# Block-sparse attention and feed-forward: P turned in f32 by TensorE, P by V in f32, values read straight from the input

## The chip, the core and the metric

The kernel runs on one core of a Trainium2 chip. TensorE (PE in the rows; its weight loads are PEld) multiplies, VectorE (DVE), ScalarE (ACT) and GpSimd (POOL) work on vectors, and SyncE (SP) issues most of the transfers. Each engine takes its instructions in the order in which they stand. The metric is the time of one execution in microseconds (us), lower is better.

## The reference

Four batches, 8 heads, 768 tokens, 64 values per head; blocks of 32 tokens, so 24 blocks. What is computed, cut to the core:

```python
scores = (q @ k.T) / 8                         # per head, 768 x 768
# allowed for a query block: itself and its two neighbours, blocks 0 and 23, 3 sampled blocks;
# query blocks 0 and 23 see everything
scores = where(mask, scores, -1e9); scores -= max(scores, -1)
attn = exp(scores); attn /= sum(attn, -1) + 1e-9
x = (attn @ v)                                 # 768 x 512 per batch, heads side by side
xn = (x - mean(x)) / sqrt(var(x) + 1e-6) * g   # over the 512
out = x + relu(xn @ w_ch1) @ w_ch2             # 512 -> 2048 -> 512, f32
```

## The kernel before, in words

**Tiles and visits.** A batch is six tiles of 128 query tokens, taken in the order 1, 2, 3, 0, 4, 5. Tile 0 holds the query blocks 1, 2, 0 and 23. Each other tile is worked in two visits of kind N (four heads each; 4 heads x 256 keys = 1024 columns of scores). Tile 0 takes four visits of kind D (two heads, the two blocks that see all 768 keys) and one of kind H (all eight heads for the other two blocks). That makes 15 visits a batch, 60 in all: 40 N, 16 D, 4 H.

**A step.** The loop at the end of the function runs one step per visit. In step s it writes, in this order: the scores of visit s (`scores`, f32 matmuls into PSUM), their row maxima (`biggest`), then P by V of the visit two steps earlier (`LAG` is 2; `attn_v`, `evict`), then the exponentials of visit s (`softmax`), and then a list of tasks with pieces of the feed-forward network between them. The order of each engine's instructions is that of this writing.

**P in halves.** P is kept as a high and a low f16 part: ScalarE rounds (L278), GpSimd takes the difference (L279), and SyncE turns both by DMA transposes (`turn`, L285) into `pth` and `ptl`. V is held in the same way: at the start of each batch the values are loaded, scaled and split, and stored as f16 rows (high, a column of ones, low: 129 per head) in a scratch tensor `vsd` in DRAM. P by V then is two f16 matmuls per piece, of 129 and of 65 columns, with 32 stationary columns each, so that four of them stand side by side in the array.

**Values.** `values` gathers the rows that a visit needs from `vsd` into one of two buffers `vs`. For an N visit SyncE issues three static transfers (L184, L189) and twelve (L204) whose block numbers it has first read into registers (L147, twice). A D visit needs one transfer for two visits, an H visit twelve.

**Feed-forward.** A tile whose attention is done is normalised (`norm_a`: DVE, ACT, POOL), turned by two DMA transposes on SyncE (`norm_b`, L360 and L361), and then goes with a second tile into a unit of 192 + 96 f16 matmuls (`pu` L377, `pd` L400; each f32 product is three f16 ones). `norm_b` is written only once the unit before has written all its `pu`. A unit is due three steps (`LAG + 2` = 4 before the change) after the last visit of its second tile, and the loop spreads a unit's matmuls evenly over the steps until the next unit is due: the planner counts 109 ns per `pu` and 215 ns per `pd`, 41.57 us for a unit of two tiles. Where the next unit is four steps away that is 10.4 us a step; where the five visits of tile 0 lie between, seven steps, it is 5.9 us.

**Start.** In the steps 0 to 7 the weights arrive as f64 words and are turned into f16 pairs by DVE, ACT and POOL (`split_w1`, `split_w2`).

Of the kernel before, what the change touches and what calls it, by code (L numbers as in the profile page):

```python
# [19 lines left out]
SV = 64.0  # L20
SP_ = 4096.0
# [6 lines left out]
def sparse_attention_moe(  # L28
# [7 lines left out]
    g: bass.AP,  # L36
    w1: bass.AP,
# [14 lines left out]
    dram = ctx.enter_context(tc.tile_pool(name="dram", bufs=1, space=bass.MemoryType.DRAM))  # L52
# [50 lines left out]

    def load_v(b, c, dma):
        dma.dma_start(vr_s[:, c % 2, :], v[b, c])

    def split_v(b, c, pool=False):
        raw = vr_s[:, c % 2, :].rearrange("p (h d) -> p h d", d=D)
        row = vrow_s[c % 2]
        r = row.rearrange("p f (h e) -> p (f h) e", e=129)  # L110
        if pool:
            nc.scalar.activation(raw, raw, AF.Copy, scale=SV)
            nc.scalar.copy(r[:, :, 0:D], raw)
            nc.gpsimd.tensor_sub(r[:, :, D + 1 : 129], raw, r[:, :, 0:D])
        else:
            nc.scalar.activation(r[:, :, 0:D], raw, AF.Copy, scale=SV)
            nc.vector.scalar_tensor_tensor(out=r[:, :, D + 1 : 129], in0=raw, scalar=SV,
                                           in1=r[:, :, 0:D], op0=ALU.mult, op1=ALU.subtract)

    def save_v(b, c, dma):  # L120
        dma.dma_start(vsd[b].rearrange("f r e -> r f e")[c * P : (c + 1) * P], vrow_s[c % 2])
# [137 lines left out]
    def biggest(vi):  # L259
# [6 lines left out]
                                scalar2=math.log(SP_), op0=ALU.mult, op1=ALU.add)  # L266

    def softmax(vi):
        n, w = vi.shape
        ps, p, st = vi.ps, p_s, vi.st  # L270
        ph, pl = ph_s[vi.i % 2], pl_s[vi.i % 2]
        half = n * w if n == 1 else n * w // 2
        for lo in range(0, n * w, half):
            for h in range(lo // w, (lo + half) // w):
                nc.scalar.activation(p[:, h * w : (h + 1) * w], ps[:, h * w : (h + 1) * w],  # L275
                                     AF.Exp, bias=st[:, 4 + h : 5 + h], scale=0.125)
            s = slice(lo, lo + half)
            nc.scalar.copy(ph[:, s], p[:, s])  # L278
            nc.gpsimd.tensor_sub(pl[:, s], p[:, s], ph[:, s])  # L279

    def turn(vi, low):
        n, w = vi.shape
        c = n * w // P
        src, dst = ((ph_s, pth_s), (pl_s, ptl_s))[low]
        nc.sync.dma_start_transpose(out=dst[vi.i % 2][:, 0:c, :],  # L285
                                    in_=src[vi.i % 2][:, 0 : n * w])

    def attn_v(vi):
        pth, ptl, vs = pth_s[vi.i % 2], ptl_s[vi.i % 2], vi.vs
        pv = vi.pv = ps_v.tile([P, 1024], F32, tag="pv", name=f"pv{vi.i}")  # L290
        for n, h in enumerate(vi.heads):
            o = 512 * (n % 4 // 2) + 129 * (n % 2)
            e = 129 * (h % 4)
            rows = slice(0, 4) if vi.kind == "N" else slice(0, 2)
            nch = 6 if vi.kind == "D" else 2
            for c in range(nch):
                for low in range(2):
                    pt, w = ((pth, 129), (ptl, D + 1))[low]
                    for gg in range(4 if vi.kind == "N" else 2):
                        first = n % 2 == 0 and c == 0 and low == 0  # L300
                        last = n % 2 == 1 and c == nch - 1 and low == 1
                        j, pr = h % 2, h // 2
                        if vi.kind == "N":
                            ch, lanes, row = (2 * j + pr % 2) * 2 + c, gg, gg
                            vv = 2 * gg + c
                        elif vi.kind == "H":
                            ch, lanes, row = (2 * j + pr // 2) * 2 + c, 2 * (pr % 2) + gg, gg
                            vv = 4 * gg + 2 * c + h // 4
                        else:
                            ch, lanes, row, vv = c, 2 * (pr % 2) + gg, 2 + gg, c  # L310
                        nc.tensor.matmul(pv[32 * row : 32 * row + 32, o : o + w],  # L311
                                         pt[:, ch, 32 * lanes : 32 * lanes + 32],
                                         vs[:, vv, e : e + w],
                                         start=first, stop=last, skip_group_check=True)
            if vi.kind == "H" and n == 3:
                yield
        yield

    def evict(vi, part):
        rows = {"N": slice(0, 128), "H": slice(0, 64), "D": slice(64, 128)}[vi.kind]  # L320
        hs = vi.heads[4 * part : 4 * part + 4]
        nb, step = len(hs) // 2, hs[1] - hs[0]
        x = vi.tile.x[rows]
        if vi.kind == "D":
            x = x.rearrange("p (a j d) -> p a j d", j=2, d=D)[:, 2 * vi.hf : 2 * vi.hf + 2, hs[0] % 2, :]
        else:
            x = x[:, hs[0] * D : (hs[0] + 4) * D].rearrange("p (h d) -> p h d", d=D)
        tl = tl_s[rows, 0 : 2 * nb, :]
        rs = sm.tile([P, 2 * nb, 1], F32, tag="rs", name=f"rs{vi.i}_{part}")[rows]

        def view(lo, hi):
            u = vi.pv.rearrange("p (b e) -> p b e", b=2)[rows, 0:nb, 0:258]
            return u.rearrange("p b (h e) -> p b h e", e=129)[:, :, :, lo:hi]

        def four(a):
            return a.rearrange("p (b h) d -> p b h d", h=2)

# [236 lines left out]
    while s < NV + LAG + 2 or queue or nextu < len(units):  # L574
# [14 lines left out]
        if vi:  # L589
            softmax(vi)  # L590
# [78 lines left out]
```

## Time and profile before

| | |
|---|---|
| median of 3 runs | 994.09 us (990.64 to 998.07) |
| profiled execution, its own time | 990.98 us |
| its span, first to last instruction | 989.2 us |
| TensorE busy | 711.0 us (72%) |
| VectorE, ScalarE, GpSimd busy | 427.5, 322.9, 299.7 us |
| mean granted TensorE clock | 0.899 of full |
| moved by DMA | 138.84 MB |

The page's busy times are those of one execution; instructions that only issue a transfer or load a register do not count as busy, so SyncE has no share there and is read from its timeline (written SPq). Scores and their times carry f32 matmuls, which the trace records as two matmuls each: the 16 of an N visit appear as x32.

### The profile page before, as it was taken

What the parts mean: (1) busy time and instruction counts of PE and PEld (TensorE: products, weight loads), DVE (VectorE), ACT (ScalarE), POOL (GpSimd) and SP (SyncE); (2) the same over time, 40 slices, a digit from 0 to 9 for tenths busy, and PEclk for the clock granted to TensorE, in tenths of its full rate; (3) what the DMA queues carried; (4) which work ended last, traced back from release to release, by engine and by line L of the source; (5) the groups of instructions that cost most, each with busy time, mean ns of one, the idle gap of its engine ahead of it and who ended that gap; (6) DMA issues with size and microseconds to landing.
All of it is one profiled execution on the core that took longest, in us unless ns stands there. A gap on an engine that the chain in (4) does not pass through costs nothing.

```text
span 989.2 us, 23113 instructions
## 1 busy us (share of the span) xinstructions
PE 711.0 (72%) x8896; PEld 452.1 (46%) x8896; DVE 427.5 (43%) x1001; ACT 322.9 (33%) x631; POOL 299.7 (30%) x319
## 2 busy tenths in 40 slices
PE   1012535698468979996579799985598899875995
PEld 0001323285247455662265474842373656632853
DVE  6539468745335334453534253453353342430300
ACT  2414344454124232262233232542241322530200
POOL 2515344454221312352312213451222212330000
PEclk9999957799779989998779899996799999986998
DMA  7895678577865556589555667777555573744000
GB/s 287 170 204 119 170 201 207 122 180 162 177 140 120 127 123 141 142 168 229 118 116 109 150 118 167 178 163 174 118 125 123 125 145 90 143 114 105 9 25 11
DMA packets 221281, 138.84 MB, mean 140 GB/s; under 512 B 157491, under 2 KB 210484, under 8 KB 220148
## 3 DMA queue, kind: packets, MB, share of 16 engines
q1 hardware_dynamic: 209250, 92.50, 44.5%
q0 software_dynamic: 8080, 30.71, 10.2%
q10 hardware_dynamic: 3842, 14.16, 4.9%
q8 instruction: 70, 1.15, 0.5%
q14 instruction: 39, 0.32, 0.1%
HBM read 88.75 MB, written 12.90 MB: 103 GB/s over the span
## 4 chain that ended last, share of the span: by engine, by line
PE 27%; SPq 21%; DMA 14%; DVE 13%; issue 12%; ACT 8%; POOL 2%; DVEq 1%; ACTq 0%; POOLq 0%
PE pu L377 11%; PE pd L400 8%; SPq L204 8%; DMA ptl<-pl 7%; SPq L147 5%; PE pv L311 5%; DMA vs<-vsd 4%; SPq L285 4%; PE ps L229 3%; ACT p L275 2%; ACT ph L278 2%; DVE st L262 2%; DVE hl L388 2%; DVE ks L164 1%; ACT hh L387 1%
## 5 line engine op out<-in xcount | busy, mean ns | idle before, releaser
L377 PEld LDWEIGHTS <-w1h 128*128 128x128 f16 x1664 | 157.5, 102 | 22.2
L400 PE MATMUL pd<-w2h,hh 128*128 128x512 f16 x384 | 152.8, 398 | 2.9 <-ACT w2h L439 2.9
L400 PE MATMUL pd<-w2l,hh 128*128 128x512 f16 x384 | 151.8, 395 | 1.9 <-POOL w2l L440 1.9
L400 PE MATMUL pd<-w2h,hl 128*128 128x512 f16 x384 | 151.9, 396 | 0.0
L338 ACT COPY tl<-pv 128x256 f32<-128x256 f32 (+2 forms) x64 | 21.9, 343 | 395.9 <-PE pv L311 395.9
L311 PE MATMUL pv<-vs,pth 128*32 128x129 f16 x1792 | 87.1, 253 | 87.9 <-DMA vs<-vsd 70.3
L279 POOL TENSOR_TENSOR pl<-p,ph 128x512 f16<-128x512 f32 (+1 forms) x104 | 133.0, 1280 | 49.0 <-ACT ph L278 26.6
L343 POOL TENSOR_TENSOR x<-tl,rs 128x256 f32<-128x256 f32 (+2 forms) x64 | 35.8, 559 | 347.7 <-ACT p L275 199.8
L229 PE MATMUL ps<-ks,q 64*32 64x256 f32 x1408 | 58.0, 432 | 106.0 <-DMA q<-qT 45.2
L388 DVE SCALAR_TENSOR_TENSOR hl<-pu,hh 128x512 f16<-128x512 f32 x96 | 65.9, 690 | 155.3 <-ACT hh L387 155.0
L377 PE MATMUL pu<-xth,w1h 128*128 128x256 f16 (+1 forms) x832 | 127.0, 277 | 0.0
L377 PE MATMUL pu<-xth,w1l 128*128 128x256 f16 (+1 forms) x832 | 124.6, 274 | 0.0
L377 PE MATMUL pu<-xtl,w1h 128*128 128x256 f16 (+1 forms) x832 | 122.6, 272 | 0.0
L400 PEld LDWEIGHTS <-hh 128*128 128x128 f16 x768 | 77.1, 101 | 99.1 <-issue 17.0
L311 PEld LDWEIGHTS <-pth 128*32 128x32 f16 x1792 | 66.7, 114 | 120.5 <-DMA vs<-vsd 69.5
L311 PE MATMUL pv<-vs,ptl 128*32 128x65 f16 x1792 | 72.8, 221 | 36.3 <-DMA ptl<-pl 36.3
L275 ACT ACTIVATE p<-ps,st 128x256 f32<-128x256 f32 (+1 forms) x192 | 88.0, 505 | 32.0 <-DVE st L265 19.9
L387 ACT ACTIVATE hh<-pu 128x512 f16<-128x512 f32 x96 | 57.1, 595 | 118.2 <-PE pu L377 113.9
L262 DVE TENSOR_REDUCE st<-ps 128x4 f32<-128x1024 f32 (+1 forms) x60 | 68.9, 1149 | 48.9 <-PE ps L229 48.1
L377 PEld LDWEIGHTS <-w1l 128*128 128x128 f16 x832 | 81.0, 102 | 10.8
L229 PEld LDWEIGHTS ps<-ks,q 64*32 64x32 f32 x1408 | 24.6, 115 | 129.9 <-issue 72.2
L311 PEld LDWEIGHTS <-ptl 128*32 128x32 f16 x1792 | 60.3, 111 | 42.7 <-DMA ptl<-pl 42.4
(83 smaller groups left out, 694.4 us busy)
## 6 DMA issues: line engine op xcount, KB each, us to landing
vs<-vsd SPq DMA_DIRECT2D x488, 32.2 KB, 1.7
vs<-vsd SPq DMA_DIRECT2D x40, 387.0 KB, 4.6
vs<-vsd SPq DMA_DIRECT2D x72, 129.0 KB, 4.5
vs<-vsd SPq DMA_DIRECT2D x8, 774.0 KB
out<-ot POOLq DMA_DIRECT2D x24, 256.0 KB, 2.8
q<-qT POOLq DMA_DIRECT2D x23, 256.0 KB, 3.3
vsd<-vrow POOLq DMA_DIRECT2D x18, 258.0 KB, 4.0
vr<-v POOLq DMA_DIRECT2D x18, 256.0 KB, 4.1
```

What stands on the lines that cost most here:

```text
L147: _, vals = nc.values_load_multi_w_load_instructions(flat, engines=[eng], min_val=0, max_val=top, skip_runtime_bounds_check_because=WHY)
L204: dma.dma_start(vs[32 * r : 32 * r + 32, 2 * gg, :], s[bass.ds(reg[3 * (gg % 2) + r] * BLK, BLK), :])
L229: nc.tensor.matmul(ps[32 * part : 32 * part + 32, col : col + n], lhs[64 * row : 64 * row + 64], rhs[64 * row : 64 * row + 64], start=True ...
L262: nc.vector.tensor_reduce(out=st[:, 0:n], in_=vi.ps[:, 0 : n * w].rearrange("p (h k) -> p h k", k=w), axis=AX.X, op=ALU.max, negate=True)
L275: nc.scalar.activation(p[:, h * w : (h + 1) * w], ps[:, h * w : (h + 1) * w], AF.Exp, bias=st[:, 4 + h : 5 + h], scale=0.125)
L279: nc.gpsimd.tensor_sub(pl[:, s], p[:, s], ph[:, s])
L285: nc.sync.dma_start_transpose(out=dst[vi.i % 2][:, 0:c, :], in_=src[vi.i % 2][:, 0 : n * w])
L311: nc.tensor.matmul(pv[32 * row : 32 * row + 32, o : o + w], pt[:, ch, 32 * lanes : 32 * lanes + 32], vs[:, vv, e : e + w], start=first, st ...
L377: nc.tensor.matmul(ph[:, j * n : (j + 1) * n], w[:, ct, fs], x[:, ct, 0:n], start=m == 0, stop=m == 3 * CT - 1, skip_group_check=True)
L387: nc.scalar.activation(dh, ph, AF.Relu)
L388: nc.vector.scalar_tensor_tensor(out=dl, in0=ph, scalar=0.0, in1=dh, op0=ALU.max, op1=ALU.subtract)
L400: nc.tensor.matmul(po, x[:, f, ts], w[:, f, :], start=m == 0, stop=m == 3 * FT - 1)
```

## The change

P stays f32. After the exponentials (now written into `p` alone, with no scale of 4096) TensorE turns the 128-column pieces of P through a PSUM tile with an identity matrix, ScalarE copies them to SBUF, and P by V is one f32 matmul of 65 columns per piece. The host lays the values out as f32 rows of 65 per head with the ones in place, and `values` gathers from that input; loading, splitting and storing V is gone, and so are the low parts of P and the addition of the two sums. P by V follows its scores by one step instead of two (`LAG` 1), the first unit may start in step 4 instead of 5, the loads of q and k are issued by SyncE instead of GpSimd, the weights' staging buffers are other ones, and the feed-forward's PSUM ring has three banks instead of four.

```diff
-    HV = 4 * 129
+    HV = 4 * 65
-    NX, LAG, FFN0 = 5, 2, 5
+    NX, LAG, FFN0 = 5, 1, 4
-    ps_f = ctx.enter_context(tc.tile_pool(name="ps_f", bufs=4, space=bass.MemoryType.PSUM))
+    ps_t = ctx.enter_context(tc.tile_pool(name="ps_t", bufs=1, space=bass.MemoryType.PSUM))
+    ps_f = ctx.enter_context(tc.tile_pool(name="ps_f", bufs=3, space=bass.MemoryType.PSUM))
-    vs_s = ring("vs", 2, [P, 8, HV], F16)
+    vs_s = ring("vs", 2, [P, 8, HV], F32)
...
     def values(vi, dma):
-        src, vs = vsd[vi.b], vi.vs
+        src, vs = v[vi.b], vi.vs
...
     def softmax(vi):
         n, w = vi.shape
-        ps, p, st = vi.ps, p_s, vi.st
-        ph, pl = ph_s[vi.i % 2], pl_s[vi.i % 2]
-        half = n * w if n == 1 else n * w // 2
-        for lo in range(0, n * w, half):
-            for h in range(lo // w, (lo + half) // w):
-                nc.scalar.activation(p[:, h * w : (h + 1) * w], ps[:, h * w : (h + 1) * w],
-                                     AF.Exp, bias=st[:, 4 + h : 5 + h], scale=0.125)
-            s = slice(lo, lo + half)
-            nc.scalar.copy(ph[:, s], p[:, s])
-            nc.gpsimd.tensor_sub(pl[:, s], p[:, s], ph[:, s])
-
-    def turn(vi, low):
-        n, w = vi.shape
-        c = n * w // P
-        src, dst = ((ph_s, pth_s), (pl_s, ptl_s))[low]
-        nc.sync.dma_start_transpose(out=dst[vi.i % 2][:, 0:c, :],
-                                    in_=src[vi.i % 2][:, 0 : n * w])
+        for h in range(n):
+            hs = slice(h * w, (h + 1) * w)
+            nc.scalar.activation(p_s[:, hs], vi.ps[:, hs], AF.Exp, bias=vi.st[:, 4 + h : 5 + h],
+                                 scale=0.125)
+
+    def turn(vi):
+        pt = ps_t.tile([P, 8, P], F32, tag="pt", name=f"pt{vi.i}")
+        c = vi.shape[0] * vi.shape[1] // P
+        dst = pt_s[vi.i % 2]
+        for lo in range(0, c, 4):
+            hi = min(c, lo + 4)
+            for k in range(lo, hi):
+                nc.tensor.transpose(pt[:, k, :], p_s[:, k * P : (k + 1) * P], id_sb)
+            nc.scalar.copy(dst[:, lo:hi, :], pt[:, lo:hi, :])
 
     def attn_v(vi):
...
+        def mm(row, col, ch, vv, e, c):
+            nc.tensor.matmul(pv[32 * row : 32 * row + 32, 65 * col : 65 * col + 65],
+                             pt[:, ch, 32 * row : 32 * row + 32], vs[:, vv, 65 * e : 65 * e + 65],
+                             start=row not in begun, stop=c == nch - 1, skip_group_check=True)
+            begun.add(row)
...
     def evict(vi):
...
-        nc.scalar.copy(four(tl), view(D + 1, 129))
...
-        nc.vector.tensor_add(four(tl), view(0, D), four(tl))
-        nc.gpsimd.tensor_mul(x, tl, rs.to_broadcast(list(x.shape)))
+            nc.vector.tensor_mul(o, u[:, :, 0:D], rs.to_broadcast([P, 4, D]))
...
-    for c in range(6):
-        at(0, first_v, c)
...
-        at(s, load_q, t.n, nc.gpsimd)
+        at(s, load_q, t.n, nc.sync)
...
-                at(s, load_k, t.b, lo, lo + 12, nc.gpsimd)
+                at(s, load_k, t.b, lo, lo + 12, nc.sync)
...
-            at(s1 - 8 + c, load_v, b, c, nc.gpsimd)
-            at(s1 - 7 + c, split_v, b, c)
-            at(s1 - 7 + c, save_v, b, c, nc.gpsimd)
...
         if vi:
+            for _ in values(vi, nc.sync):
+                pass
             softmax(vi)
...
         if vi:
-            vals = values(vi, nc.sync)
-            if s >= LAG:
-                extra = [(lambda: next(vals), ()), (lambda: turn(vi, 0), ()),
-                         (lambda: next(vals, 0), ()), (lambda: turn(vi, 1), ())]
-                tasks = extra[:2] + [(norms, ())] + extra[2:] + tasks
...
+            k = len(tasks) // 2
+            tasks = tasks[:k] + [(turn, (vi,))] + tasks[k:]
         tasks.append((norms, ()))
```

What this does to the order of two engines, in a step of an N visit. On TensorE, where the scores of a step begin before the change (`ps` are scores, `pv` P by V, `pu` and `pd` the feed-forward):

```order
L377 MATMUL pu_14_5483<-xth,w1h 128x256
L229 MATMUL ps_5486<-ks_79,q_92 32x256 x16
L311 LDWEIGHTS pth_89
L311 MATMUL pv_5506<-vs_81,pth_89 32x129
...
L311 LDWEIGHTS ptl_91
L311 MATMUL pv_5506<-vs_81,ptl_91 32x65
```

The same place in the changed kernel, and behind the dots the middle of the step before it ends:

```order
L372 MATMUL pd_4792<-w2l,hh 128x512
L257 MATMUL pt_4968<-id_sb,p 128x128 x8
L372 LDWEIGHTS hh
...
L204 MATMUL ps_5003<-ks_81,q_88 32x256 x16
L267 MATMUL pv_5023<-vs_82,pt_86 32x65 x32
L372 LDWEIGHTS hh
```

Sixty-four f16 matmuls of P by V became 32 f32 ones, and eight transposes of P stand in the middle of the step's feed-forward.

On SyncE, where a tile's transposes for the feed-forward stand (`xth`, `xtl`), before:

```order
L204 DMA vs_82<-vsd_117 32x516
L285 DMA_TRANSPOSE pth_88<-ph_84 128x8x128
L360 DMA_TRANSPOSE xth<-xh_100 128x4x128
L361 DMA_TRANSPOSE xtl<-xl_102 128x4x128
L147 TENSOR_LOAD ei
L204 ISA
...
L285 DMA_TRANSPOSE ptl_90<-pl_86 128x8x128
L184 DMA vs_81<-vsd_117 96x4x516
L189 DMA vs_81<-vsd_117 32x4x516 x2
```

And now:

```order
L179 DMA vs_83<-v 32x260
L130 DMA q_87<-qT 128x512
L332 DMA_TRANSPOSE xth<-xh_95 128x4x128
L333 DMA_TRANSPOSE xtl<-xl_97 128x4x128
L159 DMA vs_82<-v 96x4x260
L164 DMA vs_82<-v 32x4x260 x2
L122 TENSOR_LOAD ei
```

The transposes of P are gone from SyncE; those of the feed-forward's input stood between the two halves of a visit's gather and now stand behind the whole gather of one visit and ahead of that of the next.

## Rows read from the trace of the kernel before

**Rows 1.** The page: busy us by engine; chain that ended last, by engine.

```profile
PE 711.0 (72%) x8896; PEld 452.1 (46%) x8896; DVE 427.5 (43%) x1001; ACT 322.9 (33%) x631; POOL 299.7 (30%) x319
...
PE 27%; SPq 21%; DMA 14%; DVE 13%; issue 12%; ACT 8%; POOL 2%; DVEq 1%; ACTq 0%; POOLq 0%
```

**Rows 2.** Busy us by stretch: length, engines (instructions), TensorE clock, DMA share, GB/s.

```profile
0.00:94.21 94.21, 12.37 (x257) 6.03 (x257) 54.76 (x103) 33.19 (x54) 38.29 (x32) 1.00 0.77 200
94.21:174.84 80.63, 35.85 (x564) 23.87 (x564) 54.33 (x94) 33.16 (x57) 33.81 (x28) 0.80 0.74 187
174.84:214.99 40.15, 33.16 (x348) 20.47 (x348) 25.19 (x47) 19.07 (x34) 19.17 (x21) 0.80 0.57 137
...
425.28:576.04 150.76, 115.54 (x1508) 73.23 (x1507) 62.72 (x170) 50.75 (x109) 45.93 (x54) 0.88 0.67 145
576.04:633.33 57.29, 56.03 (x671) 36.17 (x670) 24.60 (x58) 19.77 (x35) 17.74 (x21) 1.00 0.72 149
...
844.90:989.20 144.30, 111.75 (x1203) 71.79 (x1202) 32.66 (x77) 28.09 (x59) 20.23 (x24) 0.88 0.29 67
```

**Rows 3.** SyncE's timeline, 303 to 318 us: start, us, line, operation, count.

```profile
303.19 0.53 SPq L184 DMA_DIRECT2D vs<-vsd  x1
303.77 0.94 SPq L189 DMA_DIRECT2D vs<-vsd  x2
306.27 3.91 SPq L204 DMA_DIRECT2D vs<-vsd  x6
310.27 1.25 SPq L285 DMA_TRANSPOSE pth<-ph  x1
313.33 2.91 SPq L204 DMA_DIRECT2D vs<-vsd  x6
316.34 1.24 SPq L285 DMA_TRANSPOSE ptl<-pl  x1
317.67 0.53 SPq L184 DMA_DIRECT2D vs<-vsd  x1
```

**Rows 4.** TensorE's waits: for whom, us in total, times, longest.

```profile
PE pv L311 <- DMA vs<-vsd: 70.3, 35, 5.6
PE ps L229 <- DMA q<-qT: 62.8, 3, 37.0
...
PE pv L311 <- DMA ptl<-pl: 36.3, 22, 6.0
```

**Rows 5.** TensorE's timeline from 304 us, an N visit.

```profile
304.17 1.10 PE L229 MATMUL ps<-ks,q 64*32 64x256 f32 x32 [1.65 <-DVE ks L171]
305.20 0.24 PE L311 MATMUL pv<-vs,pth 128*32 128x129 f16 x4
...
306.02 0.61 PE L377 MATMUL pu<-xth,w1h 128*128 128x256 f16 x4
```

**Rows 6.** TensorE's timeline from 367 us, a D visit.

```profile
367.37 1.49 PE L229 MATMUL ps<-kx,q 64*32 64x512 f32 x16
368.79 0.24 PE L311 MATMUL pv<-vs,pth 128*32 128x129 f16 x4
```

**Rows 7.** TensorE's timeline near the end: 512 and 128 columns.

```profile
957.47 0.38 PE L400 MATMUL pd<-w2h,hl 128*128 128x512 f16 x1
957.68 0.38 PE L400 MATMUL pd<-w2l,hh 128*128 128x512 f16 x1
957.90 0.39 PE L377 MATMUL pu<-xth,w1h 128*128 128x128 f16 x4
958.12 0.39 PE L377 MATMUL pu<-xth,w1l 128*128 128x128 f16 x4
```

**Rows 8.** Timelines of a tile's normalisation (DVE first, POOL last) and of the end.

```profile
321.88 0.69 DVE L348 BATCH_NORM_STATS2 ln<-x 128x6 f32<-128x512 f32 x1 [0.73 <-POOL x L343]
...
325.21 1.24 POOL L356 TENSOR_TENSOR xl<-xn,xh 128x512 f16<-128x512 f32 x1 [0.53 <-ACT xh L355]
...
979.18 0.69 DVE L406 SCALAR_TENSOR_TENSOR ot<-pd,x 128x512 f32<-128x512 f32 x1 [9.04 <-PE pd L400]
```

**Rows 9.** Groups by line: busy us, mean ns of one.

```profile
L387 ACT ACTIVATE hh<-pu 128x512 f16<-128x512 f32 x96 | 57.1, 595 | 118.2 <-PE pu L377 113.9
L229 PE MATMUL ps<-ks,q 64*32 64x256 f32 x1408 | 58.0, 432 | 106.0 <-DMA q<-qT 45.2
L229 PEld LDWEIGHTS ps<-ks,q 64*32 64x32 f32 x1408 | 24.6, 115 | 129.9 <-issue 72.2
```

More of the change, by code (lines that the diff above doesn't have):

```diff
@@ L102, in sparse_attention_moe @@
     tf = const.tile([1, NB, NR], F32, name="tf")
[L104 to L121, printed above, removed]
     def index_a():
@@ L281, in turn @@
-    def turn(vi, low):
-        n, w = vi.shape
-        c = n * w // P
-        src, dst = ((ph_s, pth_s), (pl_s, ptl_s))[low]
-        nc.sync.dma_start_transpose(out=dst[vi.i % 2][:, 0:c, :],
-                                    in_=src[vi.i % 2][:, 0 : n * w])
-    def attn_v(vi):
[L289 to L325, printed above, removed]
-        else:
[L327 to L336, printed above, removed]
-        nc.scalar.copy(four(tl), view(D + 1, 129))
-        nc.vector.tensor_scalar(out=four(rs), in0=view(D, D + 1), scalar1=SV * SP_ * 1e-9,
-                                scalar2=None, op0=ALU.add)
-        nc.vector.reciprocal(rs, rs)
-        nc.vector.tensor_add(four(tl), view(0, D), four(tl))
-        nc.gpsimd.tensor_mul(x, tl, rs.to_broadcast(list(x.shape)))
@@ new lines, in evict @@
+    def evict(vi):
+        n = 1 if vi.kind == "D" else 4
+        u = vi.pv[:, 0 : n * 65].rearrange("p (h e) -> p h e", e=65)
+        rs = sm.tile([P, n, 1], F32, tag="rs", name=f"rs{vi.i}")
+        nc.vector.tensor_scalar(out=rs, in0=u[:, :, D : D + 1], scalar1=1e-9, scalar2=None,
+                                op0=ALU.add)
+        nc.vector.reciprocal(rs, rs)
+        x = vi.tile.x
+        if vi.kind == "N":
+            o = x[:, vi.hf * 256 : vi.hf * 256 + 256].rearrange("p (h d) -> p h d", d=D)
+            nc.vector.tensor_mul(o, u[:, :, 0:D], rs.to_broadcast([P, 4, D]))
+            return
+        for rr in range(2):
+            rows = slice(64 * rr, 64 * rr + 64)
+            if vi.kind == "D":
+                h = 4 * vi.hf + 2 * rr + vi.r % 2
+                nc.vector.tensor_scalar(out=x[64:128, h * D : (h + 1) * D], in0=u[rows, 0, 0:D],
+                                        scalar1=rs[rows, 0, :], scalar2=None, op0=ALU.mult)
+            else:
+                for pp in range(2):
+                    o = x[0:64, (4 * pp + 2 * rr) * D : (4 * pp + 2 * rr + 2) * D]
+                    nc.vector.tensor_mul(o.rearrange("p (j d) -> p j d", d=D),
+                                         u[rows, 2 * pp : 2 * pp + 2, 0:D],
+                                         rs[rows, 2 * pp : 2 * pp + 2, :].to_broadcast([64, 2, D]))
@@ L479, in sparse_attention_moe @@
                                  shape=(1, 768) if kind == "D" else (4, 256))
-            if not (kind == "D" and r % 2):
-                nv += 1
+            vi.fresh = not (kind == "D" and r % 2)
+            nv += vi.fresh
             vi.vs = vs_s[nv % 2]
@@ L584, in sparse_attention_moe @@
                 assert t.n < NX or tiles[t.n - NX].done
-            for part, _ in enumerate(attn_v(pvi)):
-                evict(pvi, part)
+            attn_v(pvi)
+            evict(pvi)
             if pvi is t.visits[-1]:
@@ L643 @@
     k = inputs["k"].reshape(b, h // 2, 2, 24, blk, d).transpose(0, 2, 5, 3, 1, 4)
-    v = inputs["v"].transpose(0, 2, 1, 3).reshape(b, 6, 128, h * d)
+    v = inputs["v"].transpose(0, 2, 1, 3).reshape(b, s, 2, h // 2, d).transpose(0, 2, 1, 3, 4)
+    rows = _np.zeros((b, 2, s + blk, h // 2, d + 1), _np.float32)
+    rows[:, :, :s, :, :d] = v
+    rows[:, :, :s, :, d] = 1
     w1, w2 = bits(inputs["moe_w_ch1"]), bits(inputs["moe_w_ch2"])
@@ L648 @@
         "kT": _np.ascontiguousarray(k).reshape(b, 2 * d, 24, h // 2 * blk),
[L649 removed]
+        "v": rows.reshape(b, 2, s + blk, -1),
         "sampled": _np.ascontiguousarray(inputs["sampled_blocks"]).reshape(1, -1),
```

84 lines of the change are left out of this document (39 added, 45 removed).

## The prediction

> **What bounds the kernel now.** The page first: TensorE is busy 711 of 989.2 us, and the chain that ended last runs through TensorE for 27%, SyncE's queue for 21% and transfers for 14% [rows 1]. No engine holds the whole span, so I cut it into stretches where the kinds of visit change [rows 2]. The stretch of D and H visits (57.29 us for five) has TensorE busy for 56.03 at full clock: TensorE is the bound there. The stretch of ten N visits (150.76 us) has TensorE busy for 115.54 at a mean clock of 0.88: 15.1 us a visit, something else is late. The timeline of SyncE in such a visit shows what [rows 3]: from L184 at 303.19 to the next at 317.67 its items stand without a pause, 14.48 us, and what lies between the listed ones is the two register loads. Two transposes of P at 1.25 make 2.5 of it. The other 11.9 are the gather, with one slow group (3.91 for six issues against 2.91), so 10.8 in the usual case. TensorE's waits agree: 70.3 us for gathered values, 36.3 for the turned low part of P [rows 4]. In an N stretch SyncE is the bound, and TensorE waits inside the visit with the feed-forward queued behind. The start (214.99 us up to the first N visit after the H visit) is a third regime: in the steps 0 to 3 DVE is busy 54.76 of 94.21 us and TensorE only 12.37, in the steps 4 to 7 DVE 54.33 of 80.63 [rows 2]; the longest single wait of TensorE in the run, 37.0 us for q, is there [rows 4].
>
> **TensorE, visit by visit.** Scores stay: 305.20 - 304.17 = 1.03 us for an N visit [rows 5], 368.79 - 367.37 = 1.42 for a D visit [rows 6]. P by V before: 306.02 - 305.20 = 0.82 [rows 5]. After: 32 f32 matmuls of 65 columns, recorded twice like the scores, so 64 x 65 / 4 = 1040 column steps, four side by side. The D scores give the f32 price: 16 records of 384 columns on average, four side by side, are 1536 column steps in 1.42 us, 0.925 ns each. That makes 0.96 for an N or H visit, and 48 x 65 / 4 x 0.925 = 0.72 for a D visit. I charge 0.9 and 0.7: a wash. Should each record wait for its weight load it could double, 0.9 x 60 = 54 us of TensorE; the scores carry as many loads and hide them.
>
> The transposes are new: 8 in an N or H visit, 6 in a D visit, 448 in all, and no row shows one. From below, f16 matmuls of 128 columns come every (958.12 - 957.90) / 4 = 0.056 us with their weights hidden [rows 7]. From above, an f32 product of 128 columns recorded twice at 0.925 ns costs 0.24, and one that hides nothing is the mean score record and its load, 0.432 + 0.115 = 0.55 [rows 9]. I take 0.12, one f32 record of 128 columns: a copy through the identity needs one pass where the scores take two. The Trainium skill weighs in from both sides. "TensorE: Matmul & The Clock Gate", Terms, says that the transpose mode is 4 times faster for f32, which would be 0.06 by the f32 row; its Part 4 gives about 275 ns for a transpose inside a kernel, and by that the sum below would be 0.155 x 260 = 40 us longer.
>
> So an N visit costs TensorE 1.03 + 0.9 + 8 x 0.12 = 2.9 us and its share of the feed-forward: 8.7 us in steps with 5.9 of feed-forward, 13.2 in those with 10.35. D: 1.42 + 0.7 + 0.72 = 2.8.
>
> **SyncE, visit by visit.** The gather has the same number of transfers, and its rows are 1040 bytes where they were 1032: 10.8 us stay. The 2.5 us go. A tile (two N visits) still has two transposes for the feed-forward, 2.5 to 2.6, and now also the issue of q, 0.5. Per N visit that is 10.8 + 1.5 = 12.3 against 14.4 + 1.3 = 15.7 before; the 15.1 measured is a little less since the buffers let SyncE run ahead out of the D visits. By queue alone ten visits would take 123 us.
>
> **The new wait.** The gather of visit s is written at the head of step s, and the feed-forward's two transposes at its end, ahead of the next gather. Before, they stood early in the step, inside a gather. They need the normalisation, which DVE begins after the step's last piece of feed-forward and which takes 326.45 - 321.88 = 4.6 us [rows 8]. So SyncE waits for the end of a step, and the gather behind starts late; P by V of that visit and all the feed-forward behind it on TensorE wait with it. I walk a stretch from the first N visit after H, at 0, with SyncE ahead by a visit. Step 1: 8.7 us; its normalisation ends at 12.5, its transposes at 15.1, the next gather at 25.9, landed at 27.6 [rows 3]. Step 2: 8.7, to 17.4. Step 3 asks for those values at 18.4 and waits 9.2: to 35.3. Step 4 waits 2.1: to 46.1. In step 5 a second tile's transposes have pushed the gather to 52.8: 5.7 of wait and 13.2, to 65. Of the steps 6 to 10, 13.2 each, two wait 0.9 and 0.2: 132 in all. That is 8 to 9 above the queue's own 123 and 18 above TensorE's 114. I add 3 for half clock behind the long waits and 3 for slow issues like the 3.91: **138 against 150.8**.
>
> **The rest, and the sum.** A D and H stretch is TensorE's: 2 x (2.8 + 10.3) + 2 x (2.8 + 5.9) + 8.8 = 52.5 against 57.3 (its share of the feed-forward falls by 4, since `LAG` 1 moves the units a step forward, and the N steps have that work instead). The start: DVE's work stays nearly as it is, 54.8 and 54.3 us in the two halves. What goes is the chain around V (loads, splits on ACT and POOL, the round through DRAM) and the wait for q behind it on POOL. I take 70 for the steps 0 to 3 (15 of waiting for the first transfers instead of 39), 62 for 4 to 7 and 30 for 8 to 10: 162 against 215. Bounds: 190 if half of DVE's idle time stays, 148 if almost none does. The tail from the last batch's first N visit: the same four steps to 46, P by V of the last visit at 52, then the last two units, 41.6 us and 192 x 0.056 + 48 x 0.216 = 21.1 [rows 7], then 10 us from the last matmul to the end of the span [rows 8], half clock and the last wait 5: 132 against 144.3. ACT loses L278 and the copies of `tl`, and gains two PSUM copies of at most 0.6 each [rows 9]: at no cost while the feed-forward's second half of the step covers them; without that cover they would be 1.2 us a step. POOL's work on P goes, but nobody waited there for long.
>
> Before, the three batches have N stretches of 150.8 to 152.4 and D and H stretches of 57.3 to 60.3. Sum against the profiled execution, 990.98, whose span is 1.8 shorter: 162 + 3 x (138 + 52.5) + 132 + 1.8 = **867 us**, 124 less. The median of the runs is 994.09, 3 above that execution.
>
> **The rivals.**
> - *The transposes cost twice or more* (0.24 to 0.28). Only steps bound by TensorE pay: six N steps with 8 and the D and H visits with 32 a batch, some 20 in the start, 260 transposes: +31 to +42, so **898 to 909**. For it: the f32 price of the scores. Against: they need no product. 18%.
> - *The start keeps its pace*, DVE being slowed by other things than V: 190 for 162, **895**. For it: the weights' 16.8 MB (2 x 512 x 2048 x 8 bytes) still come and are split in that time. 13%.
> - *The N stretch does not shrink*: SyncE's wait for the end of the step falls on every tile with the whole gather behind it, 13.4 us from each pair of transposes on, and 150 for 138: **903**. For it: SyncE is in order and both gather buffers are then in use. 10%.
> - *Slower: the granted clock falls behind the transposes.* In the rows the clock is 1.00 where TensorE is busy for 98% of a stretch and 0.88 where it is busy for 77% [rows 2]. If the transposes worked on the clock as idle time does, the feed-forward behind them in each step would run at the lower level, 1.2 GHz: about 4.2 us a step more, 60 steps, 250 less 60 hidden under SyncE's pace: **1057**. It decides from 2.2 us lost a step (134 / 60). Against: a transpose phase is 1 us, and pauses of that length stand before full-speed work in the trace (1.65 us, then the scores in 1.03) [rows 5]. The Trainium skill's same page, Part 4, states that the full clock does not engage for transpose mode; by that this rival holds. 5%.
> - *No change: transposes that hide nothing*, 0.55 each. Then also the short N steps are TensorE's: 4 x 12.2 + 6 x 16.6 + 5 and 66 for D and H, 220 a batch; with 190 and 140 at the ends **990**. 3%.
>
> **Numbers.** The forecast itself holds 51% (840 to 885 on its own). Range 838 to 920: it takes in the three dearer cases and a transpose at 0.056 (-17). A measurement of this kernel can tell about 1% from no change. Faster by over 1%: 51 + 18 + 13 + 10 = 92%, less 1 for an overrun of several of them: 91. Within 1%: 3. Slower: 6.
>
> **What would show it.** SyncE's timeline without L285 and with pauses of several us ahead of the feed-forward's transposes; an N stretch near 138 with TensorE waiting for `vs` in the third step after H and hardly for `pt`; D and H near 52; the transposes as 448 records some 0.12 apart; the first N visit after H near 162. It is wrong if transposes stand 0.25 or more apart, if the clock row drops in D and H stretches, or if SyncE is still without pause in N stretches.

## The result and the profile after

The changed kernel took 950.83 us (median of four runs, 950.6 to 953.8); the kernel before, run beside it, 995.17. The ratio is 0.9565 (95% interval 0.9523 to 0.9607): faster by 4.3%, where 867 us, 12.5% less, had been forecast, and 950.83 lies outside the range of 838 to 920. The profiled execution took 950.94 us, its span 949.2.

The page of the changed kernel, in the views of [rows 1]: busy time by engine, then the chain that ended last.

```profile
PE 737.7 (78%) x9344; PEld 486.4 (51%) x9344; DVE 387.8 (41%) x996; ACT 283.4 (30%) x553; POOL 83.8 (9%) x80
...
issue 67%; PE 8%; SPq 7%; DMA 5%; DVE 5%; POOL 4%; ACT 3%; DVEq 0%; ACTq 0%; POOLq 0%
```

SyncE's queue fell from 21% of the chain to 7%, but what came in its place is "issue", time for which the profile names no wait. So the kernel is read by stretches, cut as in [rows 2] (start by the steps 0 to 3, 4 to 7, 8 to 10; the N stretch of the third batch; its D and H stretch; the tail):

```profile
0.00:94.26 94.26, 19.32 (x353) 10.75 (x353) 59.40 (x116) 30.06 (x44) 23.83 (x17) 0.78 0.59 180
94.26:176.98 82.72, 42.90 (x605) 28.85 (x604) 50.16 (x105) 34.56 (x63) 22.60 (x18) 0.76 0.48 144
176.98:206.63 29.65, 27.50 (x394) 21.49 (x394) 10.85 (x25) 9.81 (x18) 0.58 (x1) 1.00 0.30 76
411.17:560.59 149.42, 126.11 (x1645) 84.64 (x1644) 58.50 (x169) 45.69 (x97) 7.96 (x9) 0.94 0.46 101
560.59:618.98 58.39, 54.88 (x646) 34.54 (x645) 20.36 (x57) 15.87 (x29) 2.25 (x3) 1.00 0.32 84
822.61:949.20 126.59, 106.02 (x1132) 68.22 (x1131) 30.97 (x72) 24.32 (x50) 6.19 (x8) 0.93 0.20 47
```

| stretch, us | before | forecast | after |
|---|---|---|---|
| start, to the first N visit after H | 215.0 | 162 | 206.6 |
| N stretches (three) | 150.8 to 152.4 | 138 | 146.1, 149.4, 145.2 |
| D and H stretches | 57.3 to 60.3 | 52.5 | 58.4 |
| tail | 144.3 | 132 | 126.6 |

Of the 83.6 us between 867.3 and 950.9 the start makes 44.6, the N stretches 26.7, the D and H stretches 17.7, and the tail gives 5.4 back. In the steps 0 to 3 nothing was gained at all: 94.21 us before, 94.26 after. Against the kernel before, the span is 40.0 us shorter (989.2 to 949.2): 8.4 of it lie in the start, 13.7 in the three N stretches, 0.2 in the D and H stretches and 17.7 in the tail.

TensorE's waits after the change, to be read beside [rows 4]: for whom, total us, times, longest.

```profile
PE pt L257 <- ACT pt L258: 129.8, 60, 17.7
PE pv L267 <- DMA vs<-v: 43.9, 29, 3.2
PE ps L204 <- DVE ks L146: 15.5, 1, 15.5
```

The waits of 70.3 us for the gather and 36.3 for the turned low part are down to 43.9 together. The first line is new: in each of the 60 visits the turn waits for ScalarE, and 94.3 of its 129.8 us lie in the eleven visits of the start. Where it stands, in a short N step (the view of [rows 5]):

```profile
411.17 1.09 PE L204 MATMUL ps<-ks,q 64*32 64x256 f32 x32
412.20 1.11 PE L267 MATMUL pv<-vs,pt 128*32 128x65 f32 x64
...
415.44 0.60 PE L257 MATMUL pt<-id_sb,p 128*128 128x128 f32 x4
416.71 0.66 PE L257 MATMUL pt<-id_sb,p 128*128 128x128 f32 x4 [0.68 <-ACT pt L258]
```

Four transposes come 0.109 us apart, in 0.44 us. The next four wait for ScalarE's copy of the first four, since all eight write one PSUM tile `pt`: 1.27 us lie between the starts of the halves where 0.44 would do, 0.83 too much, with the feed-forward queued behind. The groups by line (busy us, mean ns of one, then the idle time ahead) give the operations that had no row before:

```profile
L257 PE MATMUL pt<-id_sb,p 128*128 128x128 f32 x448 | 78.2, 295 | 137.1 <-ACT pt L258 129.8
...
L267 PE MATMUL pv<-vs,pt 128*32 128x65 f32 x3584 | 79.0, 235 | 44.0 <-DMA vs<-v 43.9
L258 ACT COPY pt<-pt 128x512 f32<-128x512 f32 x120 | 67.0, 559 | 147.1 <-PE pt L257 136.1
```

In the start the same wait is up to 17.7 us long. TensorE there:

```profile
19.64 1.11 PE L257 MATMUL pt<-id_sb,p 128*128 128x128 f32 x4 [2.16 <-ACT p L247]
38.43 1.12 PE L257 MATMUL pt<-id_sb,p 128*128 128x128 f32 x4 [17.68 <-ACT pt L258]
39.48 1.96 PE L204 MATMUL ps<-ks,q 64*32 64x256 f32 x32
```

And ScalarE, for whose copy it waits:

```profile
23.25 1.05 ACT L411 CAST w1h<-stg 128x1024 f16<-128x1024 f32 x1
35.38 0.33 ACTq L393 DMA_DIRECT2D w2h<-w  x1
35.76 1.06 ACT L410 ACTIVATE stg<-stg 128x1024 f32<-128x1024 f32 x1 [11.46 <-DMA vs<-v]
36.85 1.04 ACT L411 CAST w1h<-stg 128x1024 f16<-128x1024 f32 x1
36.91 0.33 ACTq L393 DMA_DIRECT2D w2h<-w  x1
37.80 0.58 ACT L258 COPY pt<-pt 128x512 f32<-128x512 f32 x1
```

From 24.3 to 35.4 ScalarE stands at a load of weights (L393) that it issues itself. By the semaphores in the trace it is released by a transfer of the gather, whose data the load doesn't touch; why it waits for that one is not shown. Its copy of `pt` is queued behind, TensorE's second half of the turn behind the copy, the next scores behind that, and DVE's maxima behind the scores. In the steps 0 to 4 TensorE waits for that copy 17.7, 11.0, 8.3, 16.5 and 13.4 us. ScalarE's stands of this kind are only part of it: 11.5, 2.6, 0, 7.8 and 8.8 us. The rest is the conversion of the weights (L410, L411), which is written ahead of the copy as well and waits for DVE's shifts. In step 2, where ScalarE issues no load:

```profile
63.85 1.06 ACT L410 ACTIVATE stg<-stg 128x1024 f32<-128x1024 f32 x1 [2.28 <-DVE stg L405]
```

The N stretch holds the stall that was forecast. SyncE in the third batch's step 28 and at the head of step 29:

```profile
432.37 7.78 SPq L179 DMA_DIRECT2D vs<-v  x12
440.24 0.37 SPq L159 DMA_DIRECT2D vs<-v  x1
440.66 1.41 SPq L164 DMA_DIRECT2D vs<-v  x3
443.60 8.62 SPq L179 DMA_DIRECT2D vs<-v  x12
452.27 0.41 SPq L130 DMA_DIRECT2D q<-qT  x1
452.78 0.85 SPq L127 DMA_DIRECT2D kx<-kT  x2
453.72 1.52 SPq L332 DMA_TRANSPOSE xth<-xh  x1
```

Two gathers stand back to back, late, and behind them the next batch's keys (`kx`), whose load the change had moved onto this queue. TensorE is idle for 8.7, 4.9 and 3.0 us in the three steps 28 to 30, 16.6 in all, beside 17.0 in the walk of the prediction. But only 11.0 of these are waits for gathered values (8.1, 0.6 and 2.3). Another 2.0 are the turn's, and 3.6, at the end of step 29, stand ahead of the scores of step 30, whose keys DVE copied late:

```profile
461.49 0.50 DVE L139 COPY ks<-kx 128x128 f32 x3 [5.91 <-DMA kx<-kT]
```

### The profile page after: what moved, and what is told of

It is laid out like the page before. It is cut to its first block, busy times and chain, and to the rows that moved or that the text cites. A ratio compares the mean times of both kernels' runs of the same rounds, so it can differ in the third digit from the quotient of the medians.

```text
span 949.2 us, 23159 instructions
## 1 busy us (share of the span) xinstructions
PE 737.7 (78%) x9344; PEld 486.4 (51%) x9344; DVE 387.8 (41%) x996; ACT 283.4 (30%) x553; POOL 83.8 (9%) x80
## 4 chain that ended last, share of the span: by engine, by line
issue 67%; PE 8%; SPq 7%; DMA 5%; DVE 5%; POOL 4%; ACT 3%; DVEq 0%; ACTq 0%; POOLq 0%
DMA vs<-v 5%; PE pu L349 4%; SPq L179 3%; POOL xl L328 2%; SPq L122 2%; PE pt L257 1%; PE ps L204 1%; POOL out L380 1%; PE pd L372 1%; SPq L164 1%; DVE st L237 1%; ACT pt L258 1%; PE pv L267 1%; DVE ot L403 1%; ACT ot L410 1%
## 5 line engine op out<-in xcount | busy, mean ns | idle before, releaser
L257 PE MATMUL pt<-id_sb,p 128*128 128x128 f32 x448 | 78.2, 295 | 137.1 <-ACT pt L258 129.8
L247 ACT ACTIVATE p<-ps,st 128x256 f32<-128x256 f32 (+1 forms) x192 | 83.3, 510 | 262.9 <-DVE rs L296 167.8
L257 PEld LDWEIGHTS pt<-id_sb,p 128*128 128x128 f32 x448 | 51.8, 146 | 161.8 <-ACT pt L258 144.4
L267 PE MATMUL pv<-vs,pt 128*32 128x65 f32 x3584 | 79.0, 235 | 44.0 <-DMA vs<-v 43.9
L258 ACT COPY pt<-pt 128x512 f32<-128x512 f32 x120 | 67.0, 559 | 147.1 <-PE pt L257 136.1
L267 PEld LDWEIGHTS pv<-vs,pt 128*32 128x32 f32 x3584 | 64.3, 118 | 75.4 <-issue 59.8
L139 DVE COPY ks<-kx 128x128 f32 x264 | 56.3, 269 | 63.0 <-issue 42.5
L204 PE MATMUL ps<-ks,q 64*32 64x256 f32 x1408 | 53.3, 416 | 25.0 <-DVE ks L146 15.5
L378 DVE SCALAR_TENSOR_TENSOR ot<-pd,x 128x512 f32<-128x512 f32 x24 | 16.6, 691 | 133.8 <-PE pd L372 133.8
L328 POOL TENSOR_TENSOR xl<-xn,xh 128x512 f16<-128x512 f32 x24 | 27.6, 1151 | 458.8 <-ACT xh L327 452.8
```

The lines of the kernel that those rows point to most:

```text
L139: cp(ks[:, gg, r : r + 1, :], kx[:, bass.ds(t.reg[3 * (gg % 2) + r], 1), :])
L204: nc.tensor.matmul(ps[32 * part : 32 * part + 32, col : col + n], lhs[64 * row : 64 * row + 64], rhs[64 * row : 64 * row + 64], start=True ...
L247: nc.scalar.activation(p_s[:, hs], vi.ps[:, hs], AF.Exp, bias=vi.st[:, 4 + h : 5 + h], scale=0.125)
L257: nc.tensor.transpose(pt[:, k, :], p_s[:, k * P : (k + 1) * P], id_sb)
L258: nc.scalar.copy(dst[:, lo:hi, :], pt[:, lo:hi, :])
L267: nc.tensor.matmul(pv[32 * row : 32 * row + 32, 65 * col : 65 * col + 65], pt[:, ch, 32 * row : 32 * row + 32], vs[:, vv, 65 * e : 65 * e ...
```

## The experiments

Each kernel is the changed one with the edit shown. Spans and stretches are those of one profiled execution each; the changed kernel has 949.2.

**A PSUM tile for each half of the turn.**

```diff
-        pt = ps_t.tile([P, 8, P], F32, tag="pt", name=f"pt{vi.i}")
         for lo in range(0, c, 4):
+            pt = ps_t.tile([P, 4, P], F32, tag=f"pt{lo}", name=f"pt{vi.i}_{lo}")
-                nc.tensor.transpose(pt[:, k, :], ...
-            nc.scalar.copy(dst[:, lo:hi, :], pt[:, lo:hi, :])
+                nc.tensor.transpose(pt[:, k - lo, :], ...
+            nc.scalar.copy(dst[:, lo:hi, :], pt[:, 0 : hi - lo, :])
```

> The two halves of P's turn get a PSUM tile each, so that TensorE's second four transposes no longer wait for ScalarE's copy of the first four. Theory 'turn' (that wait is what the prediction charged at nothing, 0.7 to 0.84 us in each of 60 visits): the gap between the fourth and the fifth transpose goes from 0.7 us to about 0.1, steps of 9.9 and 14.4 us become 9.1 and 13.6, TensorE's waits on pt's copies fall from 130 us to under 70, and the time is 905 to 915 (about 40 less than 951), the start a little shorter too. Rival 'gather' (SyncE's gather sets the N stretches whatever TensorE saves): only the 20 D and H steps and the tail gain, some 16 to 20 us, 930 to 935. Rival 'nothing': the feed-forward's pace is set elsewhere, 945 to 955.

Measured: 912.48 us, ratio to before 0.9186 (0.9112 to 0.926), span 912.3. TensorE in the same step as above:

```profile
391.38 1.09 PE L204 MATMUL ps<-ks,q 64*32 64x256 f32 x32
392.40 1.12 PE L267 MATMUL pv<-vs,pt 128*32 128x65 f32 x64
...
395.65 1.04 PE L257 MATMUL pt<-id_sb,p 128*128 128x128 f32 x8
```

Eight transposes without a gap; the step takes 9.02 us for 9.91, the next scores starting at 400.40. The start is 13.0 us shorter, the D and H stretches 4.6 each (53.8, with TensorE busy in all of it), the N stretches 2.2, 5.6 and 2.3; the tail is the same. The theory "turn" holds. In the N stretches less came than 0.9 a visit: the waits for gathered values grew to 54.2 us. In the start ScalarE's copies still come late, and what is left of that wait has moved to P by V:

```profile
PE pv L267 <- ACT pt L258: 35.5, 6, 15.2
```

**The weights' loads on GpSimd.**

```diff
-            load_w1(i + 4, nc.scalar)
+            load_w1(i + 4, nc.gpsimd)
...
-            load_w2(i + 4, nc.scalar)
+            load_w2(i + 4, nc.gpsimd)
...
-        at(3, load_w2, i, nc.scalar)
+        at(3, load_w2, i, nc.gpsimd)
```

> Every load of the weights after the first four is issued by GpSimd in place of ScalarE. Theory 'start' (ScalarE, in order, stands at the issue of a load that waits for the gather's transfers, its copy of the turned P stands behind, and TensorE's second half of the turn behind that): ScalarE's pauses of 11.5 and 7.8 us at the loads go, the first N visit after H comes at 170 to 185 us in place of 206.6, the time is 915 to 930, and what follows the start stays as it was. Rival 'supply' (the start is set by the transfers of the weights and by DVE's shifts): the first N visit after H at 200 to 210, time 945 to 955. Rival 'POOL': GpSimd's subtractions of the low parts wait behind its loads, and it is slower, 955 to 975.

Measured: 936.1 us, 0.9417 (0.9334 to 0.9499), span 936.8. ScalarE in the place shown above:

```profile
26.33 1.04 ACT L411 CAST w1h<-stg 128x1024 f16<-128x1024 f32 x1
27.28 0.58 ACT L258 COPY pt<-pt 128x512 f32<-128x512 f32 x1
```

The copy of `pt` comes at 27.28 in place of 37.80. The steps 0 to 3 take 78.5 us for 94.3 and the first N visit after H comes at 190.4: 16.2 gained where 22 to 37 were expected, of which 12.4 are left in the span. The theory "start" is right on the loads' part in the wait and was too high in size: TensorE's waits for the copy of `pt` fell only from 129.8 to 103.4 us. "Supply" and "POOL" are out.

**The gather one step ahead.**

```diff
-            for _ in values(vi, nc.sync):
-                pass
+            for nx in (visits[:2] if s == 0 else visits[s + 1 : s + 2]):
+                for _ in values(nx, nc.sync):
+                    pass
```

> The gather of visit s+1 is written in step s, behind P by V of visit s-1 (whose buffer it takes), in place of at the head of step s+1. Theory 'late gather' (the gather stands behind the transposes of the normalised tile, which wait for the end of the step): TensorE's waits for gathered values fall from 44 us to under 12, the steps of 20 us (the third and fifth N step after H) become 14 to 16, N stretches 149 become 136 to 140, and the time is 915 to 925. Rival 'moved wait': SyncE stands still for as long, the wait shows in another step of the stretch, 940 to 955. Nothing of the start is expected to change by more than 5 us in either.

Measured: 923.82 us, 0.9307 (0.9233 to 0.938), span 918.7. The total is as expected, its parts are not. The waits for gathered values fell to 6.6 us, but the N stretches took 144.9, 143.4 and 143.3 for the 136 to 140 expected, and the start was 10.5 shorter, the tail 10.8. In the N stretch a wait had come into the gap that the gather left. DVE, of this kernel:

```profile
433.29 0.42 DVE L302 TENSOR_TENSOR x<-pv,rs 128x256 f32<-128x256 f32 x1
449.54 0.50 DVE L139 COPY ks<-kx 128x128 f32 x3 [15.82 <-DMA kx<-kT]
```

SyncE, of the same kernel:

```profile
433.73 8.12 SPq L179 DMA_DIRECT2D vs<-v  x12
441.90 0.41 SPq L130 DMA_DIRECT2D q<-qT  x1
442.41 0.85 SPq L127 DMA_DIRECT2D kx<-kT  x2
```

The keys of the next batch stand on SyncE behind a gather that begins once P by V of step 28 is done; DVE waits for them, and in step 29 TensorE is idle for 15.1 us, 13.5 of them ahead of the next scores.

**P by V two steps behind again.**

```diff
-    NX, LAG, FFN0 = 5, 1, 4
+    NX, LAG, FFN0 = 5, 2, 5
```

> One line: P by V follows its scores by two steps again, and the first unit of the feed-forward may start in step 5 again, the rest as in the changed kernel. If the late gather is what costs in the N stretches, a step of slack takes it away as well: N stretches 136 to 142, D and H stretches 3 to 4 longer, a tail some 5 to 10 longer, 925 to 940. If the lag of one step was a gain of its own (the shorter tail and start), it is slower than the changed kernel: 955 to 970.

Measured: 918.09 us, 0.926 (0.9182 to 0.9339), span 914.1, below what either theory gave. The N stretches took 135.3, 135.1 and 137.2 with the same keys' stall inside (TensorE's waits for `ks`: 53.0 us, 15.4 of them for the first scores of the run), the D and H stretches 63.1, 4.7 longer where 3 to 4 were expected; the tail was not longer (124.7) and the start 14.1 shorter. In the changed kernel the lag of one step was no gain: it took the gather's slack.

**Two steps of lag, and the keys loaded by GpSimd.**

```diff
-    NX, LAG, FFN0 = 5, 1, 4
+    NX, LAG, FFN0 = 5, 2, 5
...
-                at(s, load_k, t.b, lo, lo + 12, nc.sync)
+                at(s, load_k, t.b, lo, lo + 12, nc.gpsimd)
```

> P by V two steps behind, and the keys of the next batch loaded by GpSimd in place of SyncE (their loads stand behind the gathers of one or two visits on SyncE's queue). Theory 'keys behind the gather' (with two steps of lag, the three stalls of 13 to 15 us in the steps 14, 29, 44 are DVE's copy of the keys, which waits for these loads): the steps of 22 to 23 us become 9 to 11, TensorE's waits for ks fall from 53 us to under 20, the time is 875 to 885, 35 to 42 less than the 918 of two steps of lag alone. Rival 'gather again': the stall moves to gathered values in the same step, 905 to 920. Rival 'traffic': the loads take as long from another queue, 900 to 920.

Measured: 898.14 us, 0.9037 (0.8964 to 0.9111), span 895.0: 19 to 20 less than two steps of lag alone, half of what was expected. The waits for `ks` did fall from 53.0 to 15.2 us, and the steps 14, 29 and 44 from 22 or 23 to 14.5 to 14.9. What is left there is another transfer of the same queue, as TensorE's waits show (the first line is the wait for the first scores of the run):

```profile
PE ps L204 <- DVE ks L146: 15.2, 1, 15.2
PE ps L204 <- DMA q<-qT: 14.8, 5, 4.7
```

**The keys alone on GpSimd** (the second part of that edit, by itself).

> The changed kernel with one piece undone: the next batch's keys are loaded by GpSimd again. With P by V one step behind, the gather's stall and the keys' wait stand in the same steps. Theory 'hidden behind the gather': only the last 3.6 us of the keys' wait show ahead of the scores of the visits 15, 30, 45, and half clock behind them: 10 to 20 us less than 951, 930 to 942. Rival 'nothing' (the gather's stall fills what the keys leave): 945 to 953.

Measured: 943.64 us, 0.9431 (0.9401 to 0.9461), span 943.9: 5 to 7 less, between the two theories. With the late gather in place the keys' wait is mostly covered. So of what the change did to the keys' loads little shows in its own time; it becomes the bound once the gather is early.

**Every transpose twice.**

```diff
-                nc.tensor.transpose(pt[:, k, :], ...
+                for _ in range(2):
+                    nc.tensor.transpose(pt[:, k, :], ...
```

> Every transpose of P is written twice, the rest as in the changed kernel. Theory 'cadence' (a transpose costs TensorE what lies between the starts of two, 0.109 us, not what its record says, 0.295): 8 x 0.109 = 0.87 us a visit, 9.9 and 14.4 us steps become 10.8 and 15.3, the whole is 35 to 49 us longer than 951 (the steps that wait for the gather may hide some): 985 to 1000. Rival 'record' (0.295 each): 448 x 0.295 = 132 us, 1070 to 1085. Rival 'hidden': nothing changes where TensorE is not the bound, 950 to 970. If a longer turn dropped the granted clock behind it, the clock of a D and H stretch would leave 1.00 and the time would be above 1085.

Measured: 984.33 us, 0.9889 (0.9811 to 0.9968), span 985.0, 33 to 36 us more than the changed kernel and just below the 985 to 1000 of "cadence". "Record" and "hidden" are out. A D and H stretch, which has 32 transposes (24 in the D visits, 8 in the H visit), took 61.77 for 58.39 us: 3.38 / 32 = 0.106 us each. Its window:

```profile
579.84:641.61 61.77, 58.39 (x678) 38.05 (x678) 20.35 (x57) 15.98 (x29) 2.25 (x3) 1.00 0.29 80
```

The granted clock there is 1.00, the higher of its two levels, with 64 transposes in five steps.

**SyncE's queue time back.** A constant f16 tile is turned twice a visit by DMA transposes, where the turn of P stands; nothing uses the result.

```diff
...
         dst = pt_s[vi.i % 2]
+        for j in range(2):
+            nc.sync.dma_start_transpose(out=wt_s[j][:, 0:c, :], in_=w_s[:, 0 : c * P])
```

> Two DMA transposes of a constant tile stand on SyncE's queue in every visit, where the turn of P now stands: the queue time that the change took off SyncE, with nobody waiting for what they bring. Theory 'queue' (that time is what the change gained in the N stretches): 2.5 us a visit on top of 12.3 make 14.8, more than the 14.4 of a long step and 9.9 of a short one, so the stall behind the normalised tile's transposes grows: N stretches 160 to 175 in place of 149, D and H stretches as they are, 985 to 1030. Rival 'slack' (SyncE stands still so long for other engines that 2.5 us a visit vanish): N stretches 149 to 152, 950 to 965.

Measured: 1007.75 us, 1.0085 (1.0055 to 1.0114), span 1006.0: 0.9% slower than the kernel before. The N stretches took 157.4, 157.0 and 157.1, somewhat below the 160 expected, and 19.4 more came in the start and 6.5 in the tail, which had not been named. "Slack" is out. An N stretch and the D and H stretch behind it:

```profile
441.82:598.79 156.97, 130.63 (x1644) 87.19 (x1643) 58.58 (x169) 45.69 (x97) 7.97 (x9) 0.92 0.62 125
598.79:657.33 58.54, 55.04 (x646) 34.72 (x646) 20.42 (x57) 15.86 (x29) 2.25 (x3) 1.00 0.60 130
```

The edit brings traffic as well as queue time. In the D and H stretch the DMA share rose from 0.32 to 0.60 and the time stayed at 58.5, so there the traffic cost nothing; in the N stretches and the start the two were not separated.

**Four edits together**, with two steps of lag (first) or with the gather one step ahead (second); in both the two PSUM tiles, and the weights and keys loaded by GpSimd.

> All four edits at once: a PSUM tile for each half of the turn, the weights' loads on GpSimd, P by V two steps behind, the next batch's keys loaded by GpSimd. Theory 'separate waits' (each edit takes a wait of its own, so that the gains add where they lie in different places): first N visit after H at 160 to 180 us, N stretches 115 to 122, D and H stretches 58 to 60, a tail of 120 to 125: 805 to 840. Rival 'one slack' (two steps of lag already cover what the other edits cover): 865 to 885. Below that bound the span can't come, since TensorE has 726 us of work at full clock and waits 15 us for its first transfers.

> The same four edits, but with P by V one step behind and the gather written one step ahead in place of two steps of lag. The gather then has about as much slack, and the units of the feed-forward keep the places that they have in the changed kernel. Theory 'separate waits': first N visit after H at 160 to 180, N stretches 120 to 128, D and H stretches 54, tail 112 to 118: 800 to 840, within 15 us of two steps of lag. Rival 'one slack': 865 to 885.

Measured: 854.73 us, 0.8604 (0.8532 to 0.8677), span 850.1, and 849.29 us, 0.8529 (0.8459 to 0.86), span 848.2. Both lie above the 840 at which "separate waits" ended, and below "one slack". The gains do nearly add: 36.9 (two tiles), 12.4 (weights' loads), 35.1 (lag) and 19.1 (keys behind lag) off 949.2 make 845.7, for a span of 850.1 with two steps of lag. What was too low is the expectation, which had no measured gain of the keys. The second is the better of the two by 5 us and beats both kernels: once the gather is early, a lag of one step is no loss. Its windows, cut as the table above:

```profile
0.00:69.74 69.74, 21.50 (x352) 14.48 (x352) 52.02 (x104) 24.89 (x39) 20.64 (x19) 0.74 0.72 223
69.74:149.97 80.23, 50.18 (x606) 32.79 (x605) 63.28 (x118) 38.69 (x68) 36.31 (x36) 0.76 0.57 167
...
364.47:494.59 130.12, 122.12 (x1645) 83.30 (x1644) 58.34 (x169) 44.84 (x97) 9.06 (x11) 0.97 0.51 122
494.59:548.38 53.79, 53.79 (x646) 34.63 (x645) 20.36 (x57) 15.29 (x29) 2.25 (x3) 1.00 0.30 77
730.01:848.20 118.19, 103.13 (x1132) 66.90 (x1131) 30.86 (x72) 24.05 (x50) 6.19 (x8) 0.98 0.23 51
```

In the batches TensorE now is the bound nearly everywhere; 8 us of idle time in an N stretch and the first 150 us are left.

## Why the prediction was wrong

**The step that failed** is the one on ScalarE's new work: "gains two PSUM copies of at most 0.6 each: at no cost while the feed-forward's second half of the step covers them". The size of a copy was right (0.559 us). The cover was not: it stands behind the second four transposes in TensorE's order, and these wait for the first copy. So a visit behind the start pays 0.83 us (0.89 by the step without the wait), and the price named for the case without cover, 1.2 a step, was too high, but of the right order. With a tile for each half the span is 36.9 us shorter, the largest gain of any single edit. The order of instructions shown ahead of the prediction folded the eight transposes into one row; that a copy stood between them was to be read in the diff of `turn`, together with the one tile.

**The start**, 162 forecast, 206.6 measured, is in part the same step in another place, and the largest term. The working there was that the chain around V goes and that 15 us of waiting for the first transfers stay. V's chain did go, but the turn put a new one in: TensorE waits for ScalarE, which works in order and has its own loads of the weights and their conversion ahead of the copy. Both stood on ScalarE before the change as well; new is that TensorE waits behind them. Each by itself, two tiles for the turn give 13.0 us back, the loads moved off ScalarE 16.2 and two steps of lag 14.1; all four edits together give 34.9 (171.7, with two steps of lag), so these gains overlap. A copy written ahead of the conversion was not tried. The last 10 us to the forecast are not explained. The rival "the start keeps its pace" had the right place and, with 190 us, still too little; its cause, DVE slowed by other things, is at most a small part: DVE is busy for 59.4 us in the steps 0 to 3 where 54.8 were assumed, and waits 17.8 us there for scores.

**D and H stretches**, 52.5 forecast, 58.4 measured: 4.6 of the 5.9 are the turn's wait, as the kernel with two tiles shows (53.8, TensorE busy throughout). Of the other 1.3, P by V in f32 has about half: 1.05 us for the 0.9 charged for an N or H visit and 0.82 for the 0.7 of a D visit. (The scores were said to carry as many weight loads; they carry half as many, 32 to 64 in an N visit. The doubling that was feared didn't come all the same.)

**N stretches**, 138 forecast, 146.9 on average measured. The new wait behind the normalised tile's transposes came in the steps forecast. That the idle time is of the size forecast, 16.6 us for 17.0, is partly luck: the walk had all of it as waits for gathered values, and these were 11.0. (Two slips in the walk are small: its 1.7 us to the landing stand in no row of [rows 3], and the terms of a short step add up to 8.8, not 8.7.) What was missing is the turn's wait in the steps that don't stall, and half clock behind the stalls: step 30 took 20.4 us with only 3.0 idle, 17.4 of work at a mean granted clock of 0.77, where a long step has 13.7; 3 us a stretch had been charged for half clock. The rival "the N stretch does not shrink" had 150, and it came near that, though not by the way it gave.

**SyncE.** That its queue bound the N stretches before is supported by the kernel with two dummy transposes a visit: its N stretches, 157.0 to 157.4, are longer than those before, 150.8 to 152.4. It is 57 us above the changed kernel, 30.7 of them in the N stretches. That the whole gain is what the queue gave back, less what the turn took, is not shown: the N stretches hold only 13.7 of the 40.0 us of the span. The queue times that the prediction set side by side, 15.7 a visit before and 12.3 after, count one slow group of issues before and none after; without it the first is 14.6.

**Transposes** were charged 0.12 us and cost 0.106 to 0.109. The rivals on their price (0.24 and 0.55) are out, and so is the one on the granted clock. By the record's 0.295 the price would have been nearly three times as high. On this the Trainium skill ("TensorE: Matmul & The Clock Gate", Part 4) gives about 275 ns for a bf16 transpose inside a kernel; the f32 records here agree with that as a duration, but not as a cost in a row of transposes, where the starts decide. Its sentence that the full clock does not engage for transposes was not tried here on transposes alone; among the matmuls of a D and H stretch the clock stayed at 1.00, with 32 and with 64 of them.

**The tail** was 5.4 us better than forecast. The terms given for it add up to 129.7, not to 132, and one of them, 10 us from the last matmul to the end of the span, was 5.3. DVE after the last matmul, in a span that ends at 949.2:

```profile
943.89 0.69 DVE L378 SCALAR_TENSOR_TENSOR ot<-pd,x 128x512 f32<-128x512 f32 x1 [9.04 <-PE pd L372]
```

What shortened the tail by 17.7 us against the kernel before was not tried.

## What to carry to other kernels

When a product is turned on the matrix engine in pieces, look for what stands between the pieces in that engine's order: a copy out of a PSUM tile that the next piece writes is a wait in every visit, and a second tile takes it away. Before an operation is put on an engine "at no cost", list what stands ahead of it on that engine, the transfers that it issues included, and who waits behind it. A wait that is freed uncovers the next transfer on the same queue (here gathered values, then keys, then q), so price edits together.

## What the runs showed of the hardware that was not expected

- An f32 transpose of 128 x 128 has a record of 272 ns at the least and 295 in the mean, and the next starts 109 ns later at a granted clock of 1.00, 213 ns later at 0.50 (at 55 us, in the start): the transposes of a row overlap.
- A weight load issued by ScalarE waited some 11 us and was released, by the semaphores in the trace, by a transfer of SyncE's gather, with no data in common; with the load issued by GpSimd, the copy behind it came 10.5 us earlier (27.28 for 37.80).
- Twice the DMA share (0.32 to 0.60) left a stretch that TensorE bounds as long as it was (58.4 and 58.5 us).
